# A first quad by pairs of heads, early decay weights by segments, and a table of ranks in a planned attention and mixer kernel

## The chip, the core and the metric

The kernel runs on one core of one Trainium2 chip. The metric is device time of one execution in microseconds (us). Times come from several runs; the profile is of one further execution of the same program, with every instruction's start and end. Engines are PE (TensorE's matmuls), PEld (its weight loads, which run beside matmuls), DVE (VectorE), ACT (ScalarE), POOL (GpSimd) and SP (the queue that issues most stores).

## What is computed

Eight batches, eight heads, sequence 576, head width 64, all float32 in and out. First attention with a decay that each position accumulates, then a mixer over tokens and channels.

```python
scores = scale * np.matmul(q, k.transpose(0, 1, 3, 2))
causal = np.triu(np.ones((S, S), dtype=bool), k=1)
cum = np.cumsum(np.maximum(s, 0.0), axis=-1)
bias = -(cum[:, :, :, None] - cum[:, :, None, :])
scores = np.where(causal, -1000000000.0, scores + np.minimum(bias, 0.0))
attn = softmax(scores)
x = np.matmul(attn, v)                       # heads side by side: (8, 576, 512)
...
h = np.maximum(xt @ w_tok1, 0.0) @ w_tok2    # tokens: 576 -> 256 -> 576
u = x + h.transpose(0, 2, 1)
out = u + np.maximum(u @ w_ch1, 0.0) @ w_ch2 # channels: 512 -> 1536 -> 512
```

## The kernel before

The decay is split into a factor of the key: V and a column of ones are multiplied by exp(cum - half of the last cum), and the quotient of the two products is the softmax. Only the two diagonals of 128-blocks nearest to the main one are computed; a flag that is worked out beside it chooses a general routine when the data would not allow this (they do).

Work is made of operations with an engine or a choice of engines, a duration, buffers that are read and written, and a rank (`prio`). `Plan.run` walks through time with these durations and, for each engine, picks among the operations that could start now the one of the lowest rank. What comes out is a fixed order of instructions per engine; on the chip an instruction waits for its data, and all behind it on the same engine wait with it. Buffers come from rings (4 PSUM tiles `pmx`, 2 double ones `psc`, 4 of `E`, 4 of `qT` and of `kT`, 5 of `qkn`, 2 of `vf`). Gaps of TensorE that the plan leaves in the first 45 us are filled with matmuls on a tile of zeros (line 1229).

For each batch there are two quads of four heads (`quad`). A quad's q and k come with 64 groups of 9 positions on partitions 0 to 63 for heads 0 and 2 (or 4 and 6) and on 64 to 127 for heads 1 and 3; TensorE turns them (lines 736 and 744), ACT or DVE evicts them into `qT` and `kT` (757, 759). A `pair` then handles two heads: scores (792), exp on ACT (812) into E, the products with weighted V (875), and their quotient into x (891, 897, 908). In batch 0 the causal mask is preset in PSUM by matmuls (783).

In the startup, K and Q of the first quad come in float32 by SP's queue into the space of a later buffer and are cast (546, 548). All s follow on SP; DVE clips them (554) and sums them along the row (556, one scan over 576), ACT takes the exp (562), TensorE turns it by six transposes (582) and DVE copies it to `wT` (586), which holds the weights of all batches. The merges (653) multiply V by wT into `vp`. All other loads are casting or plain DMAs issued in one chain on POOL's queue (482, 635, 918); each is issued when the eighth before it has landed, and for some stretch (`PACED`) a one-element read (`touch`, 462) also holds back the queue until the fifth before has landed.

`tok(b)` is the token part: x times w1 (975), relu (987, 989), times w2 (1037), plus x into u (1044). The channel part `chan(b)` needs u turned. From batch 2 on, a DMA turns it (1053); for batch 1 TensorE does (1062, evicted by 1070); for batch 0 the turned u is made directly in PSUM, in two halves of 256 tokens: x turned by matmuls with the identity (1003) and h added by matmuls that give it turned (1013), evicted by 1025. `chan` multiplies by w_ch1 (1093), applies relu (1100, 1102), multiplies by w_ch2 (1118), adds u (1126) and stores by SP (1131).

TensorE's ranks are of the form below: four units for a batch, attention ahead of the channel part of the batch before it.

```python
rank = 4 * (b + 1) + LAG
np_ = (b * H + h) / 2
```

## Time and profile before

| | us |
|---|---|
| median of 3 runs | 298.59 (297.95 to 298.89) |
| the profiled execution | 298.18 |
| its span, first to last instruction | 296.2 |
| TensorE busy | 285.4 |
| DVE, ACT, POOL busy | 201.6, 191.9, 81.8 |
| mean granted clock of TensorE | 0.998 |

The page counts an engine as busy while an instruction of its runs; matmuls overlap, so the time of one (its latency) is longer than the distance to the next. In a row of the order of time, start and length of a merged run of instructions come first, then engine, line, operation, what is written and read, and the count; in brackets stands how long the engine had been idle before and what ended it. DMAs appear at the time of their issue; when they land shows only in who waited for them. The chain of waits goes back from the last instruction through whatever released each step.

### The profile page before, as it was taken

How to read it: one execution, taken by the hardware profiler on the slowest of the kernel's cores; microseconds unless marked ns; L12 is line 12 of the kernel's file. 1: busy time of each engine (PE TensorE's matmuls, PEld its weight loads, DVE VectorE, ACT ScalarE, POOL GpSimd, SP SyncE). 2: the span in 40 equal slices, each digit the busy share in tenths (PEclk: the TensorE clock that was granted, in tenths of full speed). 3: DMA queues.
4: the chain of work that ended last, by engine and by line, in shares of the span. 5: the costliest groups of instructions: out<-in, count | busy, mean ns of one | idle time of the engine just before them, and what ended most of it. 6: DMA issues, size and time to landing. Idle time of an engine off the chain costs nothing.

```text
span 296.2 us, 7117 instructions
## 1 busy us (share of the span) xinstructions
PE 285.4 (96%) x2860; PEld 168.1 (57%) x2893; DVE 201.6 (68%) x434; ACT 191.9 (65%) x303; POOL 81.8 (28%) x146
## 2 busy tenths in 40 slices
PE   8899999999999999999999999999999999999991
PEld 3478666576755455457754555457754454457550
DVE  6882899899898759977969757767878541520031
ACT  5787888779999879448983477047995266028300
POOL 8645668677260830028000000017000000000000
PEclk9999999999999999999999999999999999999999
DMA  7999999999997896269804300269904400350032
GB/s 224 226 206 208 206 210 205 201 263 195 204 202 145 167 274 119 62 135 200 158 2 100 115 35 2 55 114 188 196 6 92 123 35 2 75 155 2 2 105 80
DMA packets 38344, 39.22 MB, mean 132 GB/s; under 512 B 17600, under 2 KB 30976, under 8 KB 38304
## 3 DMA queue, kind: packets, MB, share of 16 engines
q0 software_dynamic: 17072, 24.25, 44.6%
q1 hardware_dynamic: 21232, 14.44, 18.2%
q8 instruction: 24, 0.39, 0.6%
q14 instruction: 16, 0.13, 0.2%
HBM read 40.65 MB, written 9.44 MB: 169 GB/s over the span
## 4 chain that ended last, share of the span: by engine, by line
PE 91%; DMA 2%; DVE 2%; ACT 1%; issue 1%; POOL 0%; POOLq 0%; DVEq 0%
PE pmx L1093 32%; PE pmx L1118 31%; PE pmx L1037 6%; PE psc L792 6%; PE pmx L975 6%; PE psc L875 5%; DMA qkn<-in_k_dram 2%; PE pmx L736 2%; DVE qT L759 1%; ACT x L897 1%; PE psc L783 1%; PE pmx L1013 1%; PE psc L736 0%; PE pmx L744 0%; PE pmx L1003 0%
## 5 line engine op out<-in xcount | busy, mean ns | idle before, releaser
L812 ACT ACTIVATE E<-psc 128x1024 bf16<-128x1024 f32 x64 | 62.1, 1022 | 42.6 <-PE psc L792 42.5
L1093 PEld LDWEIGHTS <-wc 128*128 128x128 bf16 x624 | 58.6, 98 | 30.5 <-issue 0.2
L1093 PE MATMUL pmx<-uTb,wc 128*128 128x320 bf16 (+2 forms) x384 | 55.4, 299 | 0.1
L1118 PE MATMUL pmx<-wc,gb 128*128 128x512 bf16 (+1 forms) x243 | 53.9, 369 | 0.6 <-issue 0.2
L1093 PE MATMUL pmx<-uTa,wc 128*128 128x512 bf16 (+1 forms) x235 | 44.8, 336 | 0.3
L1118 PE MATMUL pmx<-wc,ga 128*128 128x512 bf16 x186 | 43.8, 379 | 0.3
L1118 PEld LDWEIGHTS <-gb 128*128 128x128 bf16 x252 | 23.8, 98 | 25.1 <-issue 0.2
L669 ACT ACTIVATE junk<-qkn 128x1152 bf16<-128x1152 bf16 x32 | 37.2, 1164 | 0.4
L635 POOL DMA_DIRECT2D vf<-in_v_dram x39 | 33.6, 879 | 4.2 <-issue 2.4
L1100 ACT ACTIVATE gb<-pmx 128x320 bf16<-128x320 f32 (+2 forms) x51 | 22.1, 437 | 18.3 <-PE pmx L1093 15.0
L1100 ACT ACTIVATE ga<-pmx 128x512 bf16<-128x512 f32 (+1 forms) x48 | 24.8, 526 | 12.8 <-PE pmx L1093 12.0
L1118 PEld LDWEIGHTS <-ga 128*128 128x128 bf16 x192 | 17.9, 98 | 20.0
L653 DVE TENSOR_TENSOR vp<-vf,wT 128x512 bf16<-128x512 f32 (+1 forms) x40 | 26.5, 681 | 1.3 <-DMA vf<-in_v_dram 0.9
L462 POOL CAST seen<-uTb 1x1 f32<-1x1 bf16 x10 | 2.3, 235 | 81.2 <-DMA uTb<-ub 79.5
L875 PEld LDWEIGHTS <-E 128*128 128x128 bf16 x576 | 21.1, 97 | 5.2 <-issue 0.2
L908 DVE TENSOR_TENSOR x<-psc,rc 128x640 bf16<-128x640 f32 x28 | 22.9, 822 | 0.8
L821 DVE TENSOR_TENSOR E<-E,keep 128x512 bf16<-128x512 bf16 x56 | 22.0, 415 | 1.4 <-ACT E L812 1.4
L1102 DVE TENSOR_SCALAR gb<-pmx 128x320 bf16<-128x320 f32 (+2 forms) x45 | 21.6, 491 | 1.7 <-PE pmx L1093 1.1
L1126 DVE TENSOR_TENSOR of<-pmx,ua 128x512 f32<-128x512 f32 x16 | 11.0, 690 | 16.3 <-PE pmx L1118 16.1
L792 PEld LDWEIGHTS <-kT 64*128 64x128 bf16 x320 | 12.9, 94 | 13.7 <-issue 12.0
L792 PE MATMUL psc<-qT,kT 64*128 64x256 bf16 (+2 forms) x320 | 20.3, 250 | 0.3
L875 PE MATMUL psc<-vp,E 128*128 128x65 bf16 x522 | 20.3, 193 | 0.0
(117 smaller groups left out, 328.4 us busy)
## 6 DMA issues: line engine op xcount, KB each, us to landing
vf<-in_v_dram POOLq DMA_DIRECT2D x32, 256.0 KB, 7.9
out_dram<-of SPq DMA_DIRECT2D x31, 256.0 KB, 2.2
qkn<-in_k_dram POOLq DMA_DIRECT2D x19, 288.0 KB, 7.6
qkn<-in_q_dram POOLq DMA_DIRECT2D x19, 288.0 KB, 8.1
wc<-in_moe_w_ch_dram POOLq DMA_DIRECT2D x8, 384.0 KB, 8.2
out_dram<-of SPq DMA_DIRECT2D x10, 128.0 KB, 2.3
vf<-in_v_dram POOLq DMA_DIRECT2D x7, 128.0 KB, 7.6
gb<-in_k_dram SPq DMA_DIRECT2D x1, 576.0 KB, 3.7
```

The costliest lines, as they stand in the source:

```text
L635: nc.gpsimd.dma_start(out=vf.t[p0 : p0 + n, c, :, :], in_=v[b, :, c * 128 : c * 128 + n, :].rearrange("h p d -> p h d"))
L653: eng.tensor_tensor(out=vp.t[p0 : p0 + n, c, :, 0:D], in0=vf.t[p0 : p0 + n, c, :, :], in1=wT[p0 : p0 + n, cw, b * H : b * H + H].unsqueeze ...
L669: nc.scalar.activation(out=junk[:, :].rearrange("p (t n) -> p t n", t=2), in_=i, func=AF.Square, accum_out=sq[:, col : col + 1])
L792: nc.tensor.matmul(out=ps.t[:, hh * 512 + c0 : hh * 512 + c0 + e - a], lhsT=kT.t[hh * 64 : hh * 64 + 64, j0 : j0 + 128], rhs=qT.t[hh * 64 ...
L812: nc.scalar.activation(out=E.t[:, :, 512 * pc : 512 * pc + 512], in_=ps.t[:, :].rearrange("p (e n) -> p e n", e=2), func=AF.Exp, scale=0.125)
L821: nc.vector.tensor_tensor(out=o, in0=o, in1=keep[:, :].unsqueeze(1).unsqueeze(1).to_broadcast([128, 2, 2, 128]), op=ALU.mult)
L875: nc.tensor.matmul(out=o[:, ic, 0:DE], lhsT=E.t[:, hh, d0 : d0 + 128], rhs=vp.t[:, jc, h + 2 * hh, 0:DE], start=(jc == j_lo), stop=(jc == ic))
L908: nc.vector.tensor_tensor(out=x.t[:, :, :].rearrange("p c (g f e d) -> p g e f c d", f=2, e=2, d=D)[:, h // 4, h % 2], in0=pav2()[:, :, :, ...
L1093: nc.tensor.matmul(out=pm.t[:, 0 : e - a], lhsT=wc1[:, m, cc * 128 : cc * 128 + 128], rhs=uT.t[:, m, a:e], start=(m == 0), stop=(m == NMC ...
L1100: lambda cc=cc, pm=pm, a=a, e=e: nc.scalar.activation(out=g.t[:, cc, a:e], in_=pm.t[:, 0 : e - a], func=AF.Relu),
L1102: lambda cc=cc, pm=pm, a=a, e=e: nc.vector.tensor_scalar_max(out=g.t[:, cc, a:e], in0=pm.t[:, 0 : e - a], scalar1=0.0)),
L1118: nc.tensor.matmul(out=pm.t[:, na:ne], lhsT=g.t[:, cc, c * 128 : c * 128 + 128], rhs=wc2[:, cc, na:ne], start=(cc == 0), stop=(cc == NCC - 1))
```

## The change

1. The first quad comes by pairs of heads: SP loads only heads 0 and 2 of K and Q in float32, to be cast; heads 1 and 3 come by two casting loads at the head of POOL's chain, straight into `qkn`. Each pair is turned by operations of its own (`tr_one`), 9 transposes for the first pair and 18 narrower ones for the second, per tensor.
2. The weights of batch 0 are computed apart. Its s is loaded by ACT's queue as 72 rows (8 heads, 9 segments of 64); a scan of 64 elements runs along each row, a matmul with a 72 x 72 matrix `tri0` (built on POOL) gives each segment's offset, ACT takes the exp with this offset as bias (twice side by side, so that the turn fills both halves of the partitions), TensorE turns the result and DVE spreads it into batch 0's columns of wT.
3. s as a whole is loaded later, after the turns of the second quad; its relu waits for chunk 3 of batch 0's u; the six turns get the rank (5, 3) in place of -20.
4. Only the first half of batch 0's turned mixer input is made in PSUM. Chunks 2 and 3 of u get an early rank and are turned by TensorE as in batch 1. `chan`'s groups on the first half wait for the first half only.
5. A table `SHIFT` is added to TensorE's ranks: by stage (quad, pair, tok, chan) and batch. The plan counts TensorE at half speed before 5.5 us, DMAs as free from 5.1 in place of 6.85, the issue of a turning DMA as 1.25 in place of 0.6, and gives matmuls of `chan` 2 us more after a DMA. Turning DMAs are planned behind the last load listed before them.
6. Batch 5's first quad and V are loaded behind batch 2's turned u, with its second quad.

```diff
-PACED = (16, 44)
+PACED = (18, 46)
+SHIFT = {
+    "quad": (-3.5, -6, -1.25, -1.25, -4.5, -5.75, -7.5, -2.75),
+    "pair": (-7, -8.25, -0.25, 0.25, 0, 0, 1, -1.25),
+    "tok": (-0.5, -1.5, -4, 0, -6, 0, -1, 1.5),
+    "chan": (0, 1.25, 0, 0.75, 1, 0.5, 3.5, -1.75),
+}
+COLD = 5.5
...
+        if "PE" in alts and isinstance(prio, tuple):
+            prio = (prio[0] + self.shift, *prio[1:])
...
-        dma_free = 6.85
+        dma_free = 5.1
...
+            if e == "PE" and est < COLD:
+                occ, lat = 2 * occ, lat + occ
...
-            nc.sync.dma_start(out=stage[:, ti, :, :],
-                              in_=src[0, 0:4, :, :].rearrange("(f e) (p r) d -> (e p) f (r d)", e=2, r=R))
-        P.op({"SP": (0.6, 4.0 + 0.9 * ti, load0)}, writes=[("stage", ti)], prio=-9 + ti)
+            nc.sync.dma_start(out=stage[0:64, ti, :, :],
+                              in_=src[0, 0:4:2, :, :].rearrange("f (p r) d -> p f (r d)", r=R))
+        P.op({"SP": (0.6, 3.2 + 0.3 * ti, load0)}, writes=[("stage", ti)], prio=-9 + ti)
...
-    P.op({"SP": (0.6, 4.8, lambda: nc.sync.dma_start(out=s_sb[:, :], in_=s.rearrange("b h s -> (b h) s")))},
-         writes=["s"], prio=-7)
-    P.op(dve(576, lambda: nc.vector.tensor_scalar_max(out=s_sb[:, :], in0=s_sb[:, :], scalar1=0.0)),
+    SEG = S // 9
+    s0 = sb("s0", [72, SEG], FP32, fast)
+    c0 = sb("c0", [72, SEG], FP32, fast)
+    tri0 = sb("tri0", [72, 72], FP32, fast)
+    off0 = sb("off0", [72, 1], FP32, fast)
+    wn0 = sb("wn0", [72, 2, SEG], FP32, fast)
+    b0 = Buf(r_mx)
+    P.op({"ACT": (0.6, 1.7, lambda: nc.scalar.dma_start(out=s0[:, :], in_=s[0, :, :].rearrange("h (g j) -> (h g) j", j=SEG)))},
+         writes=["s0"], prio=-7)
+
+    def scan0():
+        nc.vector.tensor_scalar_max(out=s0[:, :], in0=s0[:, :], scalar1=0.0)
+        nc.vector.tensor_tensor_scan(out=c0[:, :], data0=one_sb[0:72, 0:SEG], data1=s0[:, :], initial=0.0,
+                                     op0=ALU.mult, op1=ALU.add)
+    P.op({"DVE": (0.45, 0.6, scan0)}, reads=["s0"], writes=["c0"], prio=-8)
+    def decay0():
+        P.op({"PE": (0.2, 0.45, lambda: nc.tensor.matmul(out=b0.t[0:72, 256:257], lhsT=tri0[:, :], rhs=c0[:, SEG - 1 : SEG],
+                                                         start=True, stop=True))},
+             reads=["c0", "tri0"], writes=[(b0, 1)], prio=(-60,))
+        P.op({"DVE": (0.15, 0.2, lambda: nc.vector.tensor_copy(out=off0[:, :], in_=b0.t[0:72, 256:257]))},
+             reads=[(b0, 1)], writes=["off0"], prio=-8)
+        P.op({"ACT": (0.3, 0.4, lambda: nc.scalar.activation(
+            out=wn0[:, :, :], in_=c0[:, :].unsqueeze(1).to_broadcast([72, 2, SEG]), func=AF.Exp, bias=off0[:, 0:1], scale=1.0))},
+            reads=["c0", "off0"], writes=["wn0"], prio=-8)
+        P.op({"PE": (0.2, 0.45, lambda: nc.tensor.transpose(out=b0.t[:, 0:72], in_=wn0[:, :, :].rearrange("p c j -> p (c j)"),
+                                                            identity=identf[:, :]))},
+             reads=["wn0", "identf"], writes=[(b0, 0)], prio=(-60,))
+
+        def spread0():
+            for p in range(2):
+                n = NJ - p
+                nc.vector.tensor_copy(
+                    out=wT[64 * p : 64 * p + 64, 0:n, 0:H].rearrange("q c h -> q h c"),
+                    in_=b0.t[64 * p : 64 * p + 64, 0:72].rearrange("q (h g) -> q h g", g=9)[:, :, p : p + 2 * n - 1 : 2])
+        P.op({"DVE": (0.35, 0.45, spread0)}, reads=[(b0, 0)], writes=["wT0"], prio=2)
+
+    late_s = P.op({"SP": (0.6, 6.0, lambda: nc.sync.dma_start(out=s_sb[:, :], in_=s.rearrange("b h s -> (b h) s")))},
+                  writes=["s"], prio=5)
+    relu_s = P.op(dve(576, lambda: nc.vector.tensor_scalar_max(out=s_sb[:, :], in0=s_sb[:, :], scalar1=0.0)),
...
     def w_turn():
-        P.op({"PE": (0.7, 1.0, w_tr)}, reads=["wn", "identf"], writes=[(bw, 0)], prio=(-20,))
+        P.op({"PE": (0.7, 1.0, w_tr)}, reads=["wn", "identf"], writes=[(bw, 0)], prio=(5, 3))
         P.op(dve(384, lambda: nc.vector.tensor_copy(
-            out=wT[:, :, :].rearrange("p c e -> p (c e)"), in_=bw.t[:, 0:384])),
+            out=wT[:, :, H:], in_=bw.t[:, 0:384].rearrange("p (c e) -> p c e", e=B * H)[:, :, H:])),
             reads=[(bw, 0)], writes=["wT"], prio=-1)
...
-            P.op(alts, reads=[(vf, c), "wT"], writes=[(vp, c)], prio=-2 if b < 3 else b * 10 + 5, lock=b < 2)
+            P.op(alts, reads=[(vf, c), "wT" if b else "wT0"], writes=[(vp, c)], prio=-2 if b < 3 else b * 10 + 5, lock=b < 2)
...
+            if b == 0 and h == 0:
+                def tr_one(e, ti=ti, pv=pv):
+                    for r in range(R):
+                        for f in range(1 + e):
+                            o = pv(e)[f * D : f * D + D, r * PR : (r + 1) * PR] if e else pv(e)[:, r * PR : (r + 1) * PR]
+                            t = nat.t[64 * e : 64 * e + 64, ti, :, :].rearrange("p f n -> p (f n)")
+                            c0 = f * R * D + r * D if e else 2 * r * D
+                            nc.tensor.transpose(out=o, in_=t[:, c0 : c0 + (D if e else 2 * D)],
+                                                identity=ident[64 * e : 64 * e + 64, 64 * e : 64 * e + 64])
+                for e in range(2):
+                    P.op({"PE": (R * 0.029, R * 0.029 + 0.21, lambda e=e, t=tr_one: t(e))},
+                         reads=([(nat, ti, "half")] if e else [(nat, ti, 0), (nat, ti, 1)]) + ["ident"],
+                         writes=[(pts[e], e)] + (["turned"] if e == 0 and ti == 0 else []), holds=[dsts[e][ti]],
+                         prio=(np_ - 30 + e, 2), mode=1)
+            else:
+                turn = P.op({"PE": (R * 0.029, R * 0.029 + 0.21, tr_wide if wide else tr)}, reads=skey + ["ident"] + pads,
+                     writes=[(pts[e], e) for e in range(2)], holds=[d[ti] for d in dsts],
+                     prio=(np_ - 2 + ti, 2) if join else (np_ - 30 * (b < 1 and h < 1), 2), mode=1, after=scores[gi - 1, ti] if join else None)
+            if b == 0 and h == 4 and ti == 1:
+                late_s.deps.add(turn)
...
-            for half in range(2):
+            for half in range(1):
...
             P.op({"PE": (2 * c_pe(512)[0], 2 * c_pe(512)[0] + 0.21, mm)}, reads=hkeys + ["w2", "w2e", "padw"],
-                 writes=[(pm, 0)], holds=[dst], prio=(rank + 0.7 if b == 0 else rank - TOK, 1))
+                 writes=[(pm, 0)], holds=[dst], prio=(rank + 0.7 if b == 0 and c not in (2, 3) else rank - TOK, 1))
...
-            P.op(dve(512, add), reads=[(pm, 0)] + xkeys, writes=[ukey], prio=0)
-
-            if b == 0 or (not odd and c == 4):
+            P.op(dve(512, add), reads=[(pm, 0)] + xkeys, writes=[ukey], prio=-2 if b == 0 and c in (2, 3) else 0)
+            if b == 0 and c == 3:
+                relu_s.deps.add(P.ops[-1])
+
+            if b == 0 and c not in (2, 3) or (not odd and c == 4):
                 continue
...
-                P.op({"SP": (0.6, 0, trd)}, reads=rk, writes=[(uT, c)],
-                     prio=0, dma=0.5)
+                o = P.op({"SP": (1.25, 0, trd)}, reads=rk, writes=[(uT, c)], prio=0, dma=0.5)
+                o.deps.add(sent[-1])
...
-                ukeys = ([(uT, c, m) for c in range(a // 128, (e + 127) // 128) for m in range(NMC) if c < 4] if b < 1 else
+                ukeys = ([(uT, c, m) for c in range(2) for m in range(NMC)] if b < 1 and a == 0 else
                          [(uT, c) for c in range(a // 128, (e + 127) // 128)])
...
-                     holds=[g], prio=(rank + (cc // 6 + 0.05 * (cc % 6) + 0.4 * (a > 0) if b < 2 else 2.0 * cc / NCC), 0))
+                     holds=[g], prio=(rank + (cc // 6 + 0.05 * (cc % 6) + 0.4 * (a > 0) if b < 2 else 2.0 * cc / NCC), 0)).late = 2.0
...
+    for ti, src in enumerate((k, q)):
+        def load_half(ti=ti, src=src):
+            nc.gpsimd.dma_start(out=first.t[64:128, ti, :, :],
+                                in_=src[0, 1:4:2, :, :].rearrange("f (p r) d -> p f (r d)", r=R))
+        load_op(load_half, [(first, ti, "half")], 0.73, prio=-3, probe=lambda ti=ti: first.t[64:65, ti, 0, 0:1])
     stage_qk(0, 4)
+
+    def make_tri0():
+        t = tri0[:, :].rearrange("p (h g) -> p h g", g=9)
+        nc.gpsimd.memset(tri0[:, :], 0.5)
+        for (base, ch, pat, fill) in ((-1, -1, [[9, 8], [1, 9]], -0.5), (0, 1, [[-9, 8], [0, 9]], 0.0),
+                                      (8, -1, [[9, 8], [0, 9]], 0.0)):
+            nc.gpsimd.affine_select(out=t, in_=t, compare_op=ALU.is_ge, fill=fill, base=base, pattern=pat,
+                                    channel_multiplier=ch)
+    pool_first(1.0, make_tri0, "tri0")
     pool_first(0.95, lambda: make_identity(nc, identf), "identf")
+
+    decay0()
     stage_v(0, (0,))
     P.op({"DVE": (0.6, 0.7, neg_tri)}, reads=["neg0", "keep"], writes=["neg"], prio=-5)
+    stage_v(0, (1, 2, 3, 4))
     w_turn()
-    stage_v(0, (1, 2, 3, 4))
...
-    stage_qk(5, 0)
-    stage_v(5)
     for b in range(B):
         for h in range(0, H, 4):
             quad(b, h)
         st = tok(b)
         chan(b, *st)
+        P.shift = 0.0
         if b == 2:
             behind(b, st[2])
-            stage_qk(5, 4)
+            stage_in(5)
             stage_in(6)
```

32 lines of the change are left out of this document (16 added, 16 removed).

## The prediction

> **What bounds the kernel now.** I read the page's head and its chain of waits first, then busy time by stretches, the fill matmuls by stretches, and the order of time at both ends of the startup.
>
> ```profile
> span 296.2 us, 7117 instructions
> PE 285.4 (96%) x2860; PEld 168.1 (57%) x2893; DVE 201.6 (68%) x434; ACT 191.9 (65%) x303; POOL 81.8 (28%) x146
> PE 91%; DMA 2%; DVE 2%; ACT 1%; issue 1%; POOL 0%; POOLq 0%; DVEq 0%
> ```
>
> ```profile
> 5.40:25.15 19.75, 18.66 (x331) 12.67 (x336) 14.55 (x34) 14.97 (x28) 11.53 (x19) 1.00 1.18 215
> 25.15:45.00 19.85, 19.75 (x232) 13.87 (x232) 14.14 (x30) 16.72 (x32) 13.32 (x25) 1.00 1.12 206
> 45.00:64.00 19.00, 18.55 (x257) 12.14 (x257) 17.77 (x39) 14.74 (x21) 13.66 (x27) 1.00 1.02 225
> 64.00:290.00 226.00, 224.38 (x2041) 128.07 (x2061) 151.50 (x311) 142.44 (x222) 38.64 (x62) 1.00 0.53 111
> 290.00:296.20 6.20, 0.00 (x0) 0.00 (x0) 0.41 (x3) 0.00 (x0) 0.00 (x0) 0.89 0.13 42
> ```
>
> TensorE bounds the run: 96% busy and 91% of the chain. The columns after a stretch are its length and the busy time of PE, PEld, DVE, ACT and POOL. From 25.15, where batch 0's channel MLP starts, to 290 us TensorE idles only 0.10 + 0.45 + 1.62 = 2.17 us, and the last 6.20 us are a tail that the change leaves alone. So the change can win in three ways: start that MLP earlier, take work off TensorE, or touch the 2.17 us. Before 25.15 TensorE's share flatters it, because matmuls on zeros fill its gaps:
>
> ```profile
> 5.40:25.15 19.75, 2.69 (x10) 1.04 (x13) 1.00 1.18 215
> ```
>
> The startup in order of time (start, length, line):
>
> ```profile
> 2.49 0.83 POOL L482 DMA_DIRECT2D qkn<-in_k_dram  x1
> ...
> 4.29 0.23 POOL masks.py:199 TENSOR_SCALAR_AFFINE_SELECT identf<-identf 64x64 f32<-64x64 f32 x1
> 4.47 3.72 POOL L635 DMA_DIRECT2D vf<-in_v_dram  x4
> 4.53 0.67 ACT L548 CAST qkn<-gb 128x576 bf16<-128x576 f32 x1 [1.43 <-DMA gb<-in_k_dram]
> ...
> 6.42 0.68 ACT L548 CAST qkn<-gb 128x576 bf16<-128x576 f32 x1
> ...
> 7.49 0.44 PE L736 MATMUL pmx<-ident,qkn 64*128 64x64 bf16 x18
> ...
> 9.20 1.94 ACT L812 ACTIVATE E<-psc 128x1024 bf16<-128x1024 f32 x2 [0.61 <-PE psc L792]
> 9.57 0.37 PEld L744 LDWEIGHTS <-qkn 64*64 64x64 bf16 x36 [0.37 <-DMA qkn<-in_k_dram]
> ...
> 11.02 0.77 ACT L562 ACTIVATE wn<-cum,half 64x576 f32<-64x576 f32 x1
> ...
> 11.33 0.70 POOL L918 DMA_DIRECT2D w<-in_moe_w_tok_dram  x1 [0.80 <-DMA qkn<-in_q_dram]
> ...
> 12.01 1.42 DVE L759 COPY qT<-pmx 128x576 bf16<-128x576 bf16 x2 [0.42 <-PE pmx L744]
> ...
> 12.37 0.46 PE L582 MATMUL pmx<-identf,wn 64*128 64x64 f32 x4
> 12.54 0.71 POOL L918 DMA_DIRECT2D wc<-in_moe_w_ch_dram  x1 [0.52 <-DMA vf<-in_v_dram]
> ...
> 12.67 0.28 PE L582 MATMUL pmx<-identf,wn 64*128 64x64 f32 x2
> ...
> 13.35 0.55 DVE L586 COPY wT<-pmx 128x384 f32<-128x384 f32 x1
> ```
>
> ```profile
> 14.10 1.88 DVE L653 TENSOR_TENSOR vp<-vf,wT 128x512 bf16<-128x512 f32 x3
> ...
> 14.95 1.51 POOL L918 DMA_DIRECT2D wc<-in_moe_w_ch_dram  x2 [0.50 <-DMA vf<-in_v_dram]
> ...
> 15.41 3.06 ACT L812 ACTIVATE E<-psc 128x1024 bf16<-128x1024 f32 x3 [0.26 <-PE psc L792]
> ...
> 16.04 1.22 DVE L653 TENSOR_TENSOR vp<-vf,wT 128x512 bf16<-128x512 f32 x2
> ...
> 17.46 1.84 PE L875 MATMUL pmx<-vp,E 128*128 128x64 bf16 x54
> ...
> 21.43 1.18 PEld L975 LDWEIGHTS <-w 128*128 128x128 bf16 x19 [0.29 <-issue]
> ...
> 22.62 0.18 POOL L462 CAST seen<-wc 1x1 f32<-1x1 bf16 x1 [2.94 <-DMA wc<-in_moe_w_ch_dram]
> ```
>
> Two branches meet at the weighted V times E at 17.46: the decay weights (wT ready at 13.90, five merges into vp until 17.26), and the exps (last end 18.47). The normalised x then lets the last token matmuls start at 21.43. The DMA share is over 1.00 throughout.
>
> **Part by part: the start.** Only heads 0 and 2 come by the SP queue now, half of the bytes. K landed by 4.53 and Q by 6.42, 1.89 us apart, so half of a tensor costs about 0.95 us: K's half lands near 3.6, Q's near 4.5, against 6.42. The first pair's scores, and its exp, come up to 6.42 - 4.5 = 1.9 us earlier. The second pair waits for halves on POOL's queue; it has the 1.94 us of the first pair's exps to arrive.
>
> That is not yet the end of the startup. Heads 4 to 7 land as now: a load waits for the eighth before it, so the wait that ends at 11.33 shows Q of heads 4 to 7 landing there. Its turn, eviction and scores follow, and from 11.33 to the end of the last exp at 18.47 are 7.1 us holding five and more exps, one of 0.77 for wn, and two evictions one after the other on DVE (1.42). With pair one and wn's exp out of the way, ACT can take one eviction (0.7 saved) and lacks the 0.77: the last exp ends about 1.4 earlier, at 17.1.
>
> The other branch: batch 0's weights no longer wait for all 64 rows of s. The merges then wait for V alone. V's pieces landed at 12.5, 13.7 and 14.95, the fourth by 15.75 (the second of two issues there does not wait). One merge of 0.62 after it makes vp ready at 16.4 instead of 17.26: 0.9 earlier. The bounds of the start are thus 0.9 (V alone decides) and 1.9 (the first exp decides); I take 1.4, by the exps, which end last.
>
> Costs there: two more POOL issues (0.83 and about 0.73) and tri0, a memset and three selects of the kind that took 0.23 (some 0.9), move the first V issue from 4.47 to about 6.9. V landed 8.1 us after its issue behind queued bytes, so 2.5 us fit under that backlog; if they don't, V is 2.5 late (rival 3). The 9 further turns per tensor (18 in 0.44, 0.015 each or so beyond the first's latency), the one-column matmul and the small turn of weights lie where TensorE ran 2.69 us of fills: nothing; without that cover 0.5. s0's load precedes ACT's first work by one issue, under the wait of 1.43 for K.
>
> **The half of the mixer input.**
>
> ```profile
> 23.00 0.44 PE pmx L1013 x4
> ...
> 23.66 0.44 PE pmx L1013 x4
> ```
>
> ```profile
> 61.58 0.39 PE L1062 MATMUL pmx<-ident,ub 128*128 128x128 bf16 x4
> ```
>
> One group of x turned and h added comes every 0.66 us; two of four go: -1.32. Instead chunks 2 and 3 of u, computed anyway, are turned by 8 transposes: four of 0.219 latency end in 0.39, so 0.057 each: +0.46. Net -0.86. Their evictions (two for two) cancel. The chain mm, add, turn, eviction for the second span is covered by six groups on the first span, 24 matmuls; the 36 of line 1093 took 3.93 in the chain:
>
> ```profile
> 25.42 3.93 PE pmx L1093 x36
> ```
>
> so 2.6 us; without that cover the second span waits about 1.
>
> **The late weights.** s for the other batches, its relu, scan, exp, six turns and copy move from the startup to where TensorE is full. The turns took 12.37 to 12.95: +0.6 on TensorE. DVE gets some 2.5 us (the copy 0.55, the scan the largest) and ACT 0.77, in a stretch where (25.15 to 45) DVE is busy 14.14 and ACT 16.72 of 19.85: covered, with a bound of +1 if evictions queue behind the scan. Only batch 1's merges need them, near 41 us. SP is idle then, so the moved load delays no store.
>
> **Ranks, paces, order of loads.** These add and remove no work; they change TensorE's fixed order. Bounds: -2.17 (all idle goes) to +2 (a wait like the one below at a handful of places). I take -0.7, a third of the idle time, since the largest piece has a visible cause:
>
> ```profile
> 63.12 0.46 issue
> 63.58 0.60 ACT uTb L1070
> ```
>
> There batch 1's turned u is late and TensorE has run out of batch 0's work. Batch 5's first quad and V now issue after batch 2's turned input; POOL then idles for long (17.03 us ahead of batch 3's), so that is free:
>
> ```profile
> 125.61 0.65 POOL L462 CAST seen<-uTb 1x1 f32<-1x1 bf16 x1 [17.03 <-DMA uTb<-ub]
> ```
>
> **Sum**: -1.4 - 0.86 + 0.6 - 0.7 = -2.4 us. The profiled execution took 298.18 (span 296.2 and 2.0 around it), so 295.8 by its own time; the median shown is 298.59, 0.41 above it, so the forecast is 296.2.
>
> **A rule against the change.** POOL's first load, issued at 2.49, landed after its neighbours on SP's queue: k of heads 4 to 7 released line 744 only at 9.57. The Trainium skill, "Trainium Kernel Development and Optimization", section Key Constraints, says that DMAs from SP, ACT and POOL share the same 16 engines and interleave, so that splitting one load over queues saves only issue time. By that rule the halves on POOL's queue slow those on SP's, which is rival 2. The trace agrees only in part: Q came 1.89 us behind K although POOL's loads were already issued.
>
> **The rivals.** *1. Hidden anyway by V of batch 1.* Its products follow its last piece, which merges until 46.5:
>
> ```profile
> 45.12 1.41 DVE L653 TENSOR_TENSOR vp<-vf,wT 128x512 bf16<-128x512 f32 x2 [0.40 <-DMA vf<-in_v_dram]
> ```
>
> If batch 1's path from 46.5 to 64.2 keeps its length, TensorE dries up earlier before 64 and gives back the 1.4 and the 0.86: -2.4 + 2.26 = -0.1, 298.5. Against it: line 1118 work, and 17.7 us for a path whose own TensorE work is about half. *2. Halves interleave.* First pair no earlier; only wn's exp is gained, 0.77 for 1.4: 296.9; with the ranks worth nothing 297.6. *3. POOL's queue decides (slower).* V is issued 2.5 later. If its landing follows the issue and not the backlog, V moves from 12.5 to 15.0, vp to 17.26 - 0.9 + 2.5 = 18.9, 1.6 later than now, and the weights of the MLP behind it too: +1.6 - 0.86 + 0.6 = +1.3, 299.9. It turns into a loss, ranks aside, from a slip of 0.9 + 0.86 - 0.6 = 1.2, a first V later than 13.7. Against it: 8.1 us from issue to landing. *4. The order fits worse*: ranks at +2 and the late scan at +1: -1.66 + 3 = +1.3, 299.9. *5. All comes*: start 1.9, all 2.17 idle: -1.9 - 0.86 + 0.6 - 2.17 = -4.3, 294.3.
>
> **How the numbers follow.** Forecast (294.9 to 297.2) 0.45, rival 1 0.13, rival 2 0.10, rival 3 0.08, rival 4 0.09, rival 5 0.15. Faster by over 0.3% (below 297.7; about what this kernel's three runs can tell from no change) takes the forecast, rivals 2 and 5 and a little of rival 1: 0.72. Slower by over 0.3% (above 299.5): most of 3 and 4, 0.15. The rest, 0.13, is the same. The range reaches from 293.6, past rival 5, to 299.6, where rivals 3 and 4 begin.
>
> The row of six matmuls of line 1037 serves the next part:
>
> ```profile
> 33.02 1.40 PE pmx L1037 x6
> ```
>
> **What would show it.** First exp near 7.3 instead of 9.20; the last exp of batch 0 near 17.1; wT's batch-0 columns before V lands; first V landing still near 12.5; the first line-1093 matmul near 23.6 (25.42 - 1.4 - 1.32, and some 0.9 for u's chunks 2 and 3, now multiplied first: four matmuls of 512 columns, by that row); TensorE's idle time from there to 290 below 2.17. Wrong if that first matmul is after 24.5 us, if idle before 64 us grows by what was won, or if TensorE's busy time after the start does not fall.

## The result and the profile after

| | before | after |
|---|---|---|
| median | 298.53 us (297.95 to 299.04, 7 runs) | 300.32 us (297.98 to 300.92, 7 runs) |
| ratio, 95% interval | | 1.0051 (1.0033 to 1.0069) |
| profiled execution, its span | 298.18, 296.2 us | 299.6, 297.9 us |

The change made the kernel 0.5% slower; 296.2 had been forecast, with a range up to 299.6. The page of after, its head, busy time, granted clock in 40 slices and the chain by engine:

```profile
span 297.9 us, 7137 instructions
PE 286.2 (96%) x2865; PEld 167.9 (56%) x2898; DVE 196.9 (66%) x429; ACT 197.8 (66%) x316; POOL 84.4 (28%) x150
PEclk9799999999999999999999999999999999999996
PE 92%; DMA 2%; DVE 2%; ACT 1%; issue 1%; SPq 0%
```

Busy time by stretches of after, columns as before, with the granted clock, the DMA share and GB/s at the end:

```profile
5.40:26.58 21.18, 19.31 (x327) 12.13 (x332) 12.51 (x32) 14.99 (x28) 13.17 (x22) 0.92 1.18 215
26.58:45.00 18.42, 18.37 (x224) 13.36 (x225) 15.45 (x35) 16.05 (x28) 11.33 (x24) 1.00 1.14 202
45.00:64.00 19.00, 18.84 (x240) 11.63 (x240) 16.54 (x37) 15.74 (x22) 14.75 (x28) 1.00 1.05 208
64.00:291.20 227.20, 225.54 (x2075) 129.40 (x2096) 147.81 (x304) 148.03 (x236) 40.65 (x65) 1.00 0.52 113
291.20:297.90 6.70, 0.00 (x1) 0.00 (x0) 0.81 (x3) 0.00 (x0) 0.00 (x0) 0.65 0.15 51
```

The channel MLP of batch 0 starts at 26.58 (before: the trace has the first of those matmuls at 25.25), 1.33 later. From there to TensorE's last matmul pass 291.20 - 26.58 = 264.62 us, and before 289.87 - 25.25 = 264.62: nothing was won behind the start. The last stretch is some 0.4 longer. Together they are the 1.7 by which the span grew. So most of the loss stands in the startup, and the forecast had most of its gain there. The startup of after in order of time shows where the 1.33 arise; the mean clock of 0.92 in the first stretch is a part of it:

```profile
0.83 0.78 SPq L550 DMA_DIRECT2D gb<-in_k_dram  x1
1.67 0.61 SPq L550 DMA_DIRECT2D gb<-in_q_dram  x1
...
4.63 0.67 ACT L560 CAST qkn<-gb 64x576 bf16<-64x576 f32 x1 [0.82 <-DMA gb<-in_k_dram]
...
6.77 0.67 ACT L560 CAST qkn<-gb 64x576 bf16<-64x576 f32 x1 [1.47 <-DMA gb<-in_q_dram]
...
7.34 0.63 ACT L821 COPY kT<-pmx 128x576 bf16<-128x576 bf16 x1
...
7.66 0.42 PE L803 MATMUL pmx<-ident,qkn 64*128 64x64 bf16 x9 [0.99 <-DVE qkn L558]
...
8.12 0.76 DVE L823 COPY qT<-pmx 128x576 bf16<-128x576 bf16 x1
...
8.33 0.47 PE L803 MATMUL pmx<-ident,qkn 64*64 64x64 bf16 x18
...
9.26 0.47 PE L803 MATMUL pmx<-ident,qkn 64*64 64x64 bf16 x18
...
9.67 0.41 PE L857 MATMUL psc<-qT,kT 64*128 64x256 bf16 x4
...
10.11 1.02 ACT L877 ACTIVATE E<-psc 128x1024 bf16<-128x1024 f32 x1 [0.34 <-PE psc L857]
...
13.07 0.71 POOL L983 DMA_DIRECT2D wc<-in_moe_w_ch_dram  x1 [0.41 <-DMA vf<-in_v_dram]
...
16.22 1.83 DVE L701 TENSOR_TENSOR vp<-vf,wT 128x512 bf16<-128x512 f32 x3
16.33 3.98 ACT L877 ACTIVATE E<-psc 128x1024 bf16<-128x1024 f32 x4 [0.29 <-PE psc L857]
...
17.20 0.70 POOL L983 DMA_DIRECT2D wc<-in_moe_w_ch_dram  x1 [1.00 <-DMA vf<-in_v_dram]
...
19.17 1.90 PE L940 MATMUL pmx<-vp,E 128*128 128x64 bf16 x54
...
26.58 0.60 PE L1162 MATMUL pmx<-uTa,wc 128*128 128x256 bf16 x4
```

K's half was there at 4.63 and Q's at 6.77, where the whole tensors had come by 4.53 and 6.42. ScalarE, which takes its work in order, has Q's cast ahead of the eviction of the turned K: it stands from 5.30 until Q lands, and kT comes at 7.34 although K had been turned by 6.2. The scores do not wait for that, because qT, which they need as well, is evicted only by 8.88. TensorE idles 0.99 before Q's turn, and then its order has the two turns of the second pair (8.33 and 9.26) and a mask ahead of the first pair's scores, which start at 9.67, 0.79 after qT. In before qT was evicted by 8.74 and the scores followed at once:

```profile
8.77 0.61 PE L792 MATMUL psc<-qT,kT 64*128 64x256 bf16 x10
```

The first exp starts at 10.11 (9.20), 0.91 later: 0.35 of that is Q's cast, and the rest comes from this order. The last exp of batch 0 ends at 20.31 (18.47); between the two lies a stretch at half clock, to which the runs below come back.

### The profile page after: what moved, and what is told of

Its sections match the earlier page's. It is cut to its first block, busy times and chain, and to the rows that moved or that the text cites. A ratio compares the mean times of both kernels' runs of the same rounds, so it can differ in the third digit from the quotient of the medians.

```text
span 297.9 us, 7137 instructions
## 1 busy us (share of the span) xinstructions
PE 286.2 (96%) x2865; PEld 167.9 (56%) x2898; DVE 196.9 (66%) x429; ACT 197.8 (66%) x316; POOL 84.4 (28%) x150
## 4 chain that ended last, share of the span: by engine, by line
PE 92%; DMA 2%; DVE 2%; ACT 1%; issue 1%; SPq 0%
PE pmx L1162 32%; PE pmx L1187 31%; PE psc L857 6%; PE pmx L1103 6%; PE pmx L1041 6%; PE psc L940 5%; PE pmx L785 2%; DMA gb<-in_q_dram 2%; PE psc L848 1%; ACT x L962 1%; PE pmx L1130 1%; PE psc L785 0%; DVE kT L823 0%; PE pmx L803 0%; PE pmx L793 0%
## 5 line engine op out<-in xcount | busy, mean ns | idle before, releaser
L1162 PE MATMUL pmx<-uTb,wc 128*128 128x320 bf16 (+2 forms) x384 | 56.4, 299 | 0.1
L1169 ACT ACTIVATE gb<-pmx 128x320 bf16<-128x320 f32 (+2 forms) x62 | 26.8, 437 | 11.2 <-PE pmx L1162 7.3
L701 DVE TENSOR_TENSOR vp<-vf,wT 128x512 bf16<-128x512 f32 (+1 forms) x39 | 25.4, 683 | 1.5 <-DMA vf<-in_v_dram 1.3
L1195 DVE TENSOR_TENSOR of<-pmx,ub 128x512 f32<-128x512 f32 (+1 forms) x17 | 11.2, 660 | 16.4 <-PE pmx L1187 14.3
L771 ACT COPY qk<-qkn 128x1152 bf16<-128x1152 bf16 x18 | 20.6, 1158 | 0.0
```

The lines of the kernel that those rows point to most:

```text
L701: eng.tensor_tensor(out=vp.t[p0 : p0 + n, c, :, 0:D], in0=vf.t[p0 : p0 + n, c, :, :], in1=wT[p0 : p0 + n, cw, b * H : b * H + H].unsqueeze ...
L1162: nc.tensor.matmul(out=pm.t[:, 0 : e - a], lhsT=wc1[:, m, cc * 128 : cc * 128 + 128], rhs=uT.t[:, m, a:e], start=(m == 0), stop=(m == NMC ...
L1169: lambda cc=cc, pm=pm, a=a, e=e: nc.scalar.activation(out=g.t[:, cc, a:e], in_=pm.t[:, 0 : e - a], func=AF.Relu),
L1195: nc.vector.tensor_tensor(out=o.t[:, na:ne], in0=pm.t[:, na:ne], in1=src.t[:, si, na:ne], op=ALU.add)
```

## The experiments

### The start

**Back to whole loads (e2).** The change with its first quad loaded and turned as before (and `PACED` 16, 44).

```diff
-        dma_free = 5.1
+        dma_free = 6.56
...
-            nc.sync.dma_start(out=stage[0:64, ti, :, :],
-                              in_=src[0, 0:4:2, :, :].rearrange("f (p r) d -> p f (r d)", r=R))
+            nc.sync.dma_start(out=stage[:, ti, :, :],
+                              in_=src[0, 0:4, :, :].rearrange("(f e) (p r) d -> (e p) f (r d)", e=2, r=R))
```

> The changed kernel with the first quad loaded and turned whole by SP again, as before; decay weights by segments, half mixer input, ranks and order of loads stay. Transfer theory: the loss sits in the halves, so the first exp returns to about 9.2, the last token matmuls of batch 0 come at 21 or earlier (decay weights early, no wn exp), and the time falls to 296.5 to 297.5, below before. Rank-table theory: it stays near 300. Clock theory: the same fall as with fills, 298.5 to 299.1, if the clock holds.

298.87 us, 1.0021 (1.0008 to 1.0035). First exp at 9.24, first channel matmul at 25.09: the halves, with the order planned around them, cost 1.4 us in the whole change. The 296.5 to 297.5 of the transfer theory was missed: without the halves the rest of the change wins nothing over before. One reason is visible: the merge of the last piece of V starts only when it lands, at 17.19, and TensorE idles 0.81 us for it, so V takes back a part of the gain.

**The plan told when the halves land (e1), and POOL's halves issued later (e5).**

```diff
-        P.op({"SP": (0.6, 3.2 + 0.3 * ti, load0)}, writes=[("stage", ti)], prio=-9 + ti)
+        P.op({"SP": (0.6, 3.9 + 1.5 * ti, load0)}, writes=[("stage", ti)], prio=-9 + ti)
```

> The changed kernel, with the plan told when K's and Q's halves really land (plan figures 3.9 and 5.4 us after issue in place of 3.2 and 3.5; the profile after shows 3.8 and 5.07). Nothing else is edited; TensorE's order and its fills in the startup follow. Clock theory: the 0.99 us in which TensorE waited for Q's turn at 7.66 let the granted clock fall to half for 3.4 us; with fills there the clock stays at 1.00, the last token matmuls of batch 0 start near 21.5 to 22 instead of 23.21, and the time falls by 1.2 to 1.8, to 298.5 to 299.1. Transfer theory (Q's half lands too late, whatever TensorE does meanwhile): the time falls by less than 0.5. Rank-table theory: no change.

e5 moves the loop over `load_half` and the load of heads 4 to 7 behind the making of `tri0` and `identf`.

> The changed kernel with POOL's building of tri0 and identf ahead of its loads, so that the halves for heads 1 and 3 and all later loads are issued some 1.7 us later; the rest as it is. Sharing theory (SP's halves come late because POOL's transfers run on the same engines from 4.3 us on): Q's half lands near 5.3 to 5.7 instead of 6.74, TensorE's wait before Q's turn shrinks from 0.99 to near 0, and the clock holds in most runs; all later loads move by up to 1.7 us, so the time is not sure to fall: 299 to 301. If the halves are late for another reason (their own issue or the small load of s ahead of them), Q's half still lands at 6.5 or later.

e1: 299.81 us, 1.0047 (1.0035 to 1.0059). The startup is better (first channel matmul 25.16, although Q's half landed at 6.92, later than in after), but the new order takes 265.99 us from there to TensorE's end, 1.4 more than after's; the 298.5 to 299.1 of the clock theory was missed. So a late Q alone does not make the start worse than before's: in e1 it takes 2.95 us from Q's cast to the first exp, in after 3.34, in before 2.78. e5: 301.07, 1.0097 (1.0081 to 1.0113), just over its range; Q's half lands at 6.16, K's still only at 4.82. That is no proof that POOL's loads delay Q's half. In the nine traces of this document in which these loads stand as in after, it landed at 6.04 to 7.43 (6.17 in e3, 6.28 in e9 and e10), so 6.16 lies within the spread. Busy time while K and Q come, of before, of after and of e5:

```profile
2.40:4.60 2.20, 2.20 (x6) 0.73 (x5) 1.27 (x13) 0.77 (x2) 2.12 (x6) 1.00 1.00 374
```

```profile
2.40:4.60 2.20, 2.20 (x6) 0.76 (x5) 1.84 (x15) 1.40 (x2) 2.20 (x4) 1.00 0.98 235
```

```profile
2.40:4.60 2.20, 2.20 (x6) 0.61 (x4) 1.97 (x15) 1.40 (x2) 2.01 (x6) 1.00 0.95 248
```

The DMA engines are busy all the time (1.00, 0.98, 0.95), yet move 374 GB/s with whole tensors and 235 or 248 with halves, whether POOL's loads are beside them or not. Half of the bytes, on half of the partitions, came at under two thirds of the rate. The Trainium skill, "DMA: Bandwidth & Descriptors", section "Issuing engines are not separate DMA queues", says that loads from several engines interleave on the same 16 DMA engines. No run here shows what that costs Q's half, whose spread without any change of POOL's loads is larger than what e5 won; K's 4.82 in e5 is not explained by it.

**ScalarE's issue taken away (e16).** The small load of batch 0's s moves to SyncE, behind Q's half.

```diff
-    P.op({"ACT": (0.6, 1.7, lambda: nc.scalar.dma_start(out=s0[:, :], ...
+    P.op({"SP": (0.6, 1.7, lambda: nc.sync.dma_start(out=s0[:, :], ...
```

> The whole change, with the small load of batch 0's decay logits issued by SyncE behind Q's half instead of by ScalarE. Theory C (ScalarE's issue at the same time is what stretched SyncE's issue of K from 0.47 to 0.78 us and delays both halves): K's issue is back below 0.55, K's half lands by 4.35 (4.63) and Q's by 6.45 (6.75), the last exponential of batch 0 at 20.0 or before, time 299.0 to 300.0. Theory D (the halves are late because POOL's loads of the other halves share the DMA engines, and because packets of 64 partitions carry no more bytes at a time): K's half still lands at 4.5 to 4.7 and Q's at 6.6 to 6.9; the small load then lands later, and the time is 299.8 to 301.

304.66 us, 1.0208 (1.0185 to 1.0231), outside both expectations. K's issue is still 0.78 us and K lands at 4.78: theory C falls. The issue is 0.78 in all ten traces with halves and 0.46 or 0.47 in all with whole tensors, as in before:

```profile
0.76 0.47 SPq L538 DMA_DIRECT2D gb<-in_k_dram  x1
1.29 0.45 SPq L538 DMA_DIRECT2D gb<-in_q_dram  x1
```

The loss has another cause, in e16's order of time:

```profile
7.06 0.19 DVE L575 TENSOR_SCALAR s<-s 72x64 f32<-72x64 f32 x1 [3.32 <-DMA s<-in_s_dram]
7.29 0.29 DVE L576 TENSOR_TENSOR_SCAN c<-one_sb,s 72x64 f32<-72x64 f32 x1
7.50 1.38 DVE L558 CAST qkn<-gb 64x576 bf16<-64x576 f32 x2
...
8.36 0.63 PE L803 MATMUL pmx<-ident,qkn 64*128 64x64 bf16 x9 [3.67 <-DVE qkn L558]
```

The small load now lands at 7.06. Its clip stands ahead of both of DVE's casts, so K, there since 4.78, waits for it until 7.50, TensorE idles 3.67 us, and its clock is at half from 7.4 to 17.6 us.

**The clock (e9).** After, in its own order, with four matmuls on zeros put before Q's turn, where TensorE idled 0.99.

```diff
+        f.fn = lambda t=r_mx.tiles[slots[0]]: nc.tensor.matmul(out=t[:, :], lhsT=zero[:, 0:128], rhs=zero[:, :], start=True, stop=True)
+        fills.append(f)
```

> The changed kernel, order untouched, with four more matmuls on zeros ahead of Q's turn of the first pair, where TensorE waited from 6.67 to 7.66. Clock theory (the idle stretch drops the granted clock to half for 3.4 us, and the startup runs through it): the clock holds at 1.00 from its rise to the end, the exps of batch 0 end 1 to 1.7 us earlier than 20.30, and the time falls to 298.7 to 299.4. If the chain of ACT and DVE sets the startup whatever TensorE's clock, the exps end within 0.3 of 20.30 and the time stays at 300.

299.04 us, 1.0010 (0.9996 to 1.0024). The same stretch of startup, first of after, then of e9 (the last column but two is the clock):

```profile
9.90:13.30 3.40, 3.05 (x50) 1.30 (x47) 2.65 (x7) 2.50 (x3) 2.99 (x6) 0.50 1.10 254
```

```profile
9.90:13.30 3.40, 3.25 (x100) 1.66 (x99) 3.19 (x9) 3.34 (x5) 3.12 (x5) 1.00 1.13 260
```

In after the clock is granted in full from 6.50, at half from 9.91 to 13.33, and in full again; in e9 it holds from 4.70. TensorE gets through twice as many matmuls in that stretch. The first exp starts at 9.73, 0.53 later than in before, and yet the last one ends at 18.54 (18.47) and the first channel matmul comes at 24.81 (25.25); Q's half landed 0.49 earlier in this trace than in after's, which is a part of that. By the medians work on zeros alone is worth 300.32 - 299.04 = 1.3 us: idle time where nothing else is late is not free if it costs the clock. The single executions of after fit: the two with a mean granted clock of 0.994 and 0.996 took 297.98 and 299.22, the five with 0.981 to 0.987 took 299.6 to 300.92. The Trainium skill, "TensorE: Matmul & The Clock Gate", Part 1, describes a window of 3413 ns that runs freely, after which an idle TensorE gets half its clock. The trace agrees on the length: 13.33 - 9.91 = 3.42 us in after, 10.24, three such windows, in e16. It does not agree that the window has to be idle: in the one before the drop, 6.50 to 9.91, TensorE was busy 2.27 of 3.41 us. The same count gives 2.23 in e10 and 2.36 in e15, where the clock fell next, and 2.61 in e1, 2.87 in e9 and 3.08 in before, where it held.

### Half of the mixer input, and the plan's other edits

**The half alone on the kernel before (e4).**

```diff
-            for half in range(2):
+            for half in range(1):
```

with the ranks of chunks 2 and 3, their turns and `ukeys` as in the change.

> The kernel before with only the half of batch 0's turned mixer input left out of PSUM and chunks 2 and 3 of u turned by TensorE. By the prediction's term -0.86 us: 297.7. If the chain multiply, add, turn, evict is not covered, the second half of the channel groups waits and it is 0 to +1: 298.5 to 299.5.

297.90 us, 0.9998 (0.9978 to 1.0018), with two of its runs well above the others; by time it is undecided. The trace has the first channel matmul at 24.64 (25.25) and TensorE's last at 289.22 (289.87): 0.65 less, where 0.86 had been reckoned.

**The plan's edits and batch 5's loads alone on the kernel before (e8).**

```diff
-                P.op({"SP": (0.6, 0, trd)}, reads=rk, writes=[(uT, c)],
-                     prio=0, dma=0.5)
+                o = P.op({"SP": (1.25, 0, trd)}, reads=rk, writes=[(uT, c)], prio=0, dma=0.5)
+                o.deps.add(sent[-1])
...
-            stage_qk(5, 4)
+            stage_in(5)
```

and `late = 2.0` for `chan`.

> The kernel before with the plan's other edits alone: turning DMAs at 1.25 and behind the last load, 2 us more margin for the channel matmuls after a DMA, batch 5's first quad and V behind batch 2's turned u. By the prediction these cost nothing: 298.4. If they are what the table of zeros exposed (304.95 against 300.3), it is 2 to 5 slower.

297.48 us, 0.9964 (0.9951 to 0.9976): a gain of 1.1. TensorE's last matmul is at 290.88, later than before's 289.87; the gain is in the tail, 4.73 us instead of 6.30. This order has the flag's matmul early and before's has it last of all, which may be the reason; the next run asks that.

**The flag early in after (e10).** Rank -100 in place of 100 for that matmul.

> The changed kernel with the matmul of the flag (the last thing on TensorE's queue at 290.98, with DVE's reduction and the branch behind it) ranked ahead of the channel part. Tail theory: the 6.7 us from TensorE's end to the end of the span shrink to the 4.7 of the kernels with the plan's edits alone and with a table of zeros, whose flag is early: 1.5 to 2 us, 298.4. If the stores set the tail, no change.

299.93 us, 1.0020 (0.9996 to 1.0045), inconclusive: its profile has the clock at half from 8.2 to 15.1 and a tail of 6.08 (6.71). The tail theory had expected 4.7. The tail is only 0.6 shorter here, and that the flag explains 4.7 against 6.3 is argued from e8 and not shown; the last store of after and e10 is of 128x512, that of before and e8 of 128x256.

### The order of batch 1

**Without the table (e3), and the table alone on before (e7).**

```diff
-SHIFT = {
-    "quad": (-3.5, -6, -1.25, -1.25, -4.5, -5.75, -7.5, -2.75),
...
+SHIFT = {k: (0.0,) * 8 for k in ("quad", "pair", "tok", "chan")}
```

> The changed kernel with a table of zeros. Rank-table theory (the ranks make the fixed order worse): 1.5 to 2 us faster than the changed kernel, 298.5. Transfer and clock theories: the startup is the same, and the time is the same or up to 1 slower, 300.3 to 301.3, since TensorE idles only 1.9 us after 25 us in the changed kernel.

> The kernel before with the table of ranks alone. If the table is a gain of its own, 0 to 2 us faster (296.5 to 298.4). If it fits only the order that the whole change makes, 1 or more slower: 299.5 to 303.

e3: 304.95 us, 1.0215 (1.0176 to 1.0255), so the table is worth 4.6 us within the change. e7: 301.75, 1.0121 (1.0098 to 1.0143): on the order of before the same numbers cost 3.2. That the table made the fixed order worse, one of the theories for e3, is thus wrong within the change and right on before.

**The segments with the late weights (e6), and without them (e11), on before.** e6 is items 2 and 3 of the change, with the plan's half speed below 5.5 us; e11 has that half speed too, keeps the whole s, its scan and turns in the startup as they were and gives batch 0 its own weights.

```diff
-            P.op(alts, reads=[(vf, c), "wT"], writes=[(vp, c)], prio=-2 if b < 3 else b * 10 + 5, lock=b < 2)
+            P.op(alts, reads=[(vf, c), "wT" if b else "wT0"], writes=[(vp, c)], prio=-2 if b < 3 else b * 10 + 5, lock=b < 2)
```

> The kernel before with only the decay weights of batch 0 by segments and the late weights of the others (the plan's half speed below 5.5 us comes with it; ranks are zero, the first quad whole, the mixer input whole). By the prediction's terms: the merges stop waiting for wT, and wn's exp leaves the startup, 0.8 to 0.9 us earlier, and +0.6 for the late turns: 298.1 to 298.4. Covered-work theory fails if DVE's late relu and scan (1.8 us) hold up the evictions of the channel part: TensorE then idles more between 25 and 45 us than the 0.10 of before, and the time is 299 to 300.

> The kernel before with batch 0's decay weights by segments, while the weights of the others are made in the startup as before (load, relu, scan, exp, turns at their old ranks). Against the 302.52 with late weights: if the loss comes from the late weights (DVE's scan and the turns in the full stretch), this one has V's merges early and nothing late, 297.8 to 298.6; if it comes from the segments themselves, 301 or more.

e6: 302.52 us, 1.0130 (1.0113 to 1.0147), above both of its expectations. e11: 302.62, 1.0153 (1.0118 to 1.0188). The loss of 4 us is there without the late weights (how much of it the half speed in the plan brings was not tried apart). In e11 the weighted sums of batch 0 start at 16.25 (17.46 before), 1.2 earlier, but batch 0's last exp ends at 18.82 (18.47) and the token part behind it starts as before, 20.09 (20.05): the earlier weights win nothing. The loss lies around 45 to 70 us, where TensorE is busy 21.62 of 25.00. How batch 1's second quad goes in before (cast for the turn, turn, scores of the third and fourth pair, weighted sums):

```profile
36.76 0.89 DVE L720 COPY qk<-qkn 128x1152 bf16<-128x1152 bf16 x1
...
38.97 0.44 PE L736 MATMUL psc<-ident,qk 64*128 64x64 bf16 x18
...
41.19 0.61 PE L792 MATMUL psc<-qT,kT 64*128 64x256 bf16 x10
...
44.44 0.61 PE L792 MATMUL psc<-qT,kT 64*128 64x256 bf16 x10
...
46.72 1.25 PE L875 MATMUL psc<-vp,E 128*128 128x65 bf16 x36
```

and in e11:

```profile
39.10 1.14 ACT L766 COPY qk<-qkn 128x1152 bf16<-128x1152 bf16 x1
...
40.46 0.44 PE L780 MATMUL psc<-ident,qk 64*128 64x64 bf16 x18
...
43.10 0.61 PE L837 MATMUL psc<-qT,kT 64*128 64x256 bf16 x10
...
46.24 1.25 PE L920 MATMUL psc<-vp,E 128*128 128x65 bf16 x36
...
49.53 0.71 PE L920 MATMUL psc<-vp,E 128*128 128x65 bf16 x18
...
53.22 0.61 PE L837 MATMUL psc<-qT,kT 64*128 64x256 bf16 x10
```

All of these TensorE rows use the two `psc` buffers. In e11 the cast, of rank 20 and thus behind every eviction, is planned 2.3 us later, on ScalarE; the third pair comes 1.9 later; and by the time that its exps free the buffers, the weighted sums of the first pairs can start and rank ahead. The fourth pair, which needs both buffers, comes 8.8 us later, and batch 1's first channel matmul at 69.12 in place of 64.22.

**Two numbers of the table (e13, e14, e15).** Batch 1's quads at -6 and pairs at -8.25 added to e11, alone in the change, and taken out of the change.

```diff
+SHIFT = {k: (0.0, r) + (0.0,) * 6 for k, r in (("quad", -6), ("pair", -8.25), ("tok", 0), ("chan", 0))}
```

> The segments on the kernel before (302.62 us, 1.0153), with two entries of the table alone: batch 1's quads at -6 and batch 1's pairs at -8.25. Theory A, the order of batch 1: the segments cost their 4 us because the plan puts the scores of batch 1's fourth pair near 53 us instead of 44.4, so batch 1's first channel matmul comes at 69 instead of 64.2 and TensorE runs out of batch 0's work in 45 to 70 us. The two entries pull that pair forward: its scores start at 45 or before, the first channel matmul of batch 1 at 65 or before, the idle time in 45 to 70 falls from 5.06 to under 2 us, and the time to 297.8 to 300.0 (1.000 +- 0.004). Theory B, the segments' own work (added operations on ScalarE, VectorE and TensorE, buffers held) costs it wherever the pair stands: still over 301.5, with the pair moved.

> The whole change with its table cut to the two entries of batch 1 (quads -6, pairs -8.25), all others zero; without any table it took 304.95 us (1.0215), with the whole one 300.32. Theory A (batch 1's order is nearly all that the table is worth here): 299.5 to 302.0, the fourth pair of batch 1 at 48 or before, its first channel matmul at 66 or before (72.0 without a table), from the first channel matmul to the last of TensorE at most 266.5 (270.37 without). Theory B (the table's worth is spread over its 32 numbers): over 303.

> The whole change with its table, but these two entries at zero and the other thirty as they are. Theory A: most of the 4.6 us comes back, 302.5 to 306, with batch 1's first channel matmul after 67. Theory B: 300.0 to 301.5, the first channel matmul of batch 1 near 65.

e13: 302.92 us, 1.0154 (1.0133 to 1.0176), fourth pair at 53.12. e14: 304.65, 1.0190 (1.0155 to 1.0225). e15: 301.65, 1.0102 (1.0077 to 1.0126). In e13 TensorE's order is that of e11 from its first instruction to its last, so these two numbers alone moved nothing, and theory A falls as it was put: the fourth pair is not kept by its own rank. In the whole table they are worth 1.3 us, less than theory A expected; in e15 the fourth pair stands at 48.48 without them (47.83 in after).

**One rank of the cast (e17, e18).** Since the rows above begin with a late cast, batch 1's four casts get rank -1: e17 in the change without its table, e18 in e11.

```diff
-                     reads=[(nat, ti)], writes=[(qk, 0)], prio=20, lock=True).late = 6
+                     reads=[(nat, ti)], writes=[(qk, 0)], prio=-1 if b == 1 else 20, lock=True).late = 6
```

> The whole change without its table (304.95 us, 1.0215), and one rank altered: the four casts that lay batch 1's Q and K out for turning get rank -1 instead of 20 on ScalarE and VectorE. Theory F, one buffer's turn: without the table such a cast slips behind evictions by 1 to 3 us, the turn behind it too, and a pair's scores then find the two score buffers in PSUM given to the weighted sums of the first pairs, so the fourth pair comes 9 us late and batch 1's whole path with it; neither the segments' work nor the table's 32 numbers as such matter. Then the scores of batch 1's fourth pair start at 49 us or before (56.95), its first channel matmul comes by 67.5 (72.0), the first channel matmul to the last of TensorE takes at most 267 (270.37), and the time is 300.0 to 302.5. Theory G, the table's worth is spread over later batches or the segments' work costs it: still over 303.5.

> The segments on the kernel before (302.62 us, 1.0153), with the same one rank: batch 1's four casts at -1. Theory F: the fourth pair's scores start at 46.5 us or before (53.22), batch 1's first channel matmul by 66.5 (69.12), and the time is 298.5 to 300.8. Theory G: the pair moves, and the time stays over 301.5.

e17: 298.64 us (297.17 to 301.26), 1.0006 (0.9974 to 1.0039). e18: 300.01 us, 1.0070 (1.0036 to 1.0103). Both are in theory F's ranges or below. The rows of e18, beside those of e11:

```profile
36.12 1.16 ACT L766 COPY qk<-qkn 128x1152 bf16<-128x1152 bf16 x1
...
39.98 0.44 PE L780 MATMUL psc<-ident,qk 64*128 64x64 bf16 x18
...
42.62 0.61 PE L837 MATMUL psc<-qT,kT 64*128 64x256 bf16 x10
...
45.87 0.61 PE L837 MATMUL psc<-qT,kT 64*128 64x256 bf16 x10
...
48.15 1.25 PE L920 MATMUL psc<-vp,E 128*128 128x65 bf16 x36
```

The fourth pair is back ahead of the weighted sums. TensorE's busy time in the stretch, e3 first, then e17:

```profile
50.00:75.00 25.00, 21.32 (x305) 14.41 (x307) 20.26 (x45) 19.67 (x30) 20.11 (x36) 0.93 1.07 217
```

```profile
50.00:75.00 25.00, 24.69 (x356) 16.32 (x355) 23.35 (x51) 21.47 (x34) 20.13 (x35) 1.00 1.11 237
```

One rank did 304.95 - 298.64 = 6.3 us, more than all 32 numbers of the table (4.6). A part of it is the clock's: in e3 TensorE was busy 1.91 of the 3.41 us before 65.04, and its clock is at half from there to 68.45. Of the segments' 4 us it took back 2.6; where the remaining 1.4 lie was not tried.

### A version that beats both (e12)

Before, with the half of the mixer input, the plan's edits, batch 5's loads and the flag early; no halves, segments or table.

> The kernel before with what paid alone: half of the mixer input (-0.5), the plan's other edits and the order of loads (-0.9), and the flag's matmul early. The first two add up to -1.4; the flag is early already in the second, so it adds 0 to -0.3: 296.7 to 297.1. If the order that the plan makes is what decides, and not the sum of edits, it lies anywhere from 296 to 299.

295.81 us, 0.9911 (0.9888 to 0.9933). First channel matmul 24.61, TensorE's last 288.99, tail 4.8. The parts alone had added up to 296.7 to 297.1; where the further 0.9 comes from was not tried.

## Why the prediction was wrong, by its own steps

*The start, -1.4.* This step failed, and it is the largest: of the 4.1 us between the forecast span (2.4 less) and the measured one (1.7 more), 3.1 lie before the first channel matmul, which was to come 1.8 earlier, at 23.6, and came 1.33 later. Its own sign of being wrong, that matmul after 24.5, came true. "K's half lands near 3.6, Q's near 4.5" took half of a tensor to cost half of the distance between K and Q. They came at 4.63 and 6.77: the DMA engines moved 235 GB/s in place of 374 while the halves came, and K's issue took 0.78 in place of 0.47. Why a half goes so slowly stays open. That POOL's loads do it, rival 2's reason, is not shown for Q, and K's half is as late without them (4.82 in e5). The prediction's row against that rule, Q 1.89 behind K although POOL's loads were already issued, could not speak to it: in the trace of before the first packet of POOL's queue starts at 5.95, when those of K and Q are through. Rival 2 had only the first pair no earlier; rival 3 alone had a later start, by V, and it was not V. What made it a loss was not priced at all: the second pair's turns, put down as nothing because fills stood there, come ahead of the first pair's scores in TensorE's order (0.79 after qT, in before 0.03), and the idle 0.99 cost TensorE its clock (1.3 us by e9). The prediction set TensorE's 2.69 us of fills down as free cover; they also hold the clock.

*The weights of batch 0.* Right that the merges would then wait for V alone (e11: 1.2 earlier, reckoned 0.9), right that the exps end last, so that this is worth nothing by itself.

*V and rival 3.* The first V landed at 13.07 (12.54), the fourth at 17.20, not the full 2.5 later; vp was ready at 18.05, still ahead of the last exp at 20.31. It did not decide in after; in e2, without the halves, TensorE idled 0.81 us for it.

*The half, -0.86.* Mechanism right, size off: 0.65 on the trace of e4; the second span waited for nothing. Batch 1's first channel matmul moves with the start (62.77 in e4, 64.22 in before), so rival 1, in which batch 1's path takes such a gain back, is not seen there.

*The late weights, +0.6.* e6 against e11 shows no loss from them (302.52, 302.62).

*Ranks, -0.7, bounds -2.17 to +2.* Both the term and its bounds failed. The 2.17 us of idle time were mostly not idle. The page of before counts 2860 matmuls and 2893 weight loads, so some matmul records are missing from it. Where a trace has them nearly even the same stretch is full or nearly so (184.57 to 185.00 in ten traces). Before first, then e18:

```profile
100.00:285.00 185.00, 183.79 (x1615) 103.04 (x1631) 117.72 (x240) 107.26 (x166) 21.51 (x36) 1.00 0.45 96
```

```profile
100.00:285.00 185.00, 185.00 (x1638) 103.26 (x1637) 118.88 (x241) 108.53 (x167) 21.65 (x36) 1.00 0.43 96
```

So there was little to win. And "these add and remove no work; they change TensorE's fixed order" was taken to bound the loss by a few waits, while one order of four pairs is worth 4 to 6 us (e3, e11, e17). The segments were costed by their operations (nothing), not by the order that the plan makes once they are in; alone they cost 4.0, and the table mends what the rest of the change upsets (e3): behind the first channel matmul the change takes what before takes (264.62 us), because two effects of 4 to 5 us cancel. Rival 4, "the order fits worse", had an order as the reason, but it put the loss on the table and on the late scan, and the table was what held it off; that its 299.9, and rival 3's, lie near the 300.32 is luck, since the 1.7 us of after lie in the start and the tail.

## What to carry to other kernels

Where a planner makes a fixed order, the cost of an added operation is the order that comes out, so read the places of the scarce buffers' users (here four pairs on two `psc`) in the new order before believing a sum of durations; an operation that its rank puts behind all others (here the cast, with 20) at the head of a path is the place to look. Do not take a transfer of half the bytes to take half the time when it covers half the partitions, and look at what stands behind its consumer on the same engine. In a startup, keep TensorE busy where it waits: here an idle microsecond cost 3.4 us at half clock, and 1.3 us of the whole.

## What the hardware showed that was not expected

- A load of half a tensor on 64 partitions took 0.78 us to issue on SyncE (0.47 whole) and landed no sooner, at 4.63 to 4.98 us in the ten traces with halves, 4.53 to 4.85 in those with whole tensors. The rows are not shorter: the packets of both are of 2304 bytes. K's took 139 ns each in the mean in after and 110 in before, and the first started at 2.40 (1.88). That the number of partitions does it was not tried by itself.
- The clock's window had another phase in each execution: among the traces with halves it was first recorded as granted in full between 3.9 and 6.5 us in seven, and in e3, e17 and e14 only at 13.8, 14.1 and 17.5. After's runs spread from 297.98 to 300.92, and its two fastest have the highest mean clock.
- In e6 a VectorE copy of `w1` that takes 0.22 us elsewhere took 1.67 us at 42.15, beside GpSimd's issue of a K load (41.95 to 42.66) and its merge of V (42.67 to 43.73). Its cause was not tried.
